# Heads that come out with tokens on partitions: batches 2 to 4 of an mLSTM cell followed by an FNet mix

## Chip, cores and metric

One core of a Trainium2 chip runs the kernel, alone. The metric is the device time of one execution in microseconds; less is better. TensorE (PE) multiplies matrices, VectorE (DVE), ScalarE (ACT) and GpSimd (POOL) work on elements, and SyncE (SP) issues the transfers, one behind the other on one queue.

## The reference

```python
B, H, S, D = 4, 8, 768, 40
for t in range(S):                       # mLSTM cell, per batch and head
    m_new  = max(f_gate[t] + m, i_gate[t])
    f_stab = exp(f_gate[t] + m - m_new);  i_stab = exp(i_gate[t] - m_new);  m = m_new
    C = f_stab * C + i_stab * outer(v[t], k[t])
    n = f_stab * n + i_stab * k[t]
    y[t] = sigmoid(o_gate[t]) * (C @ q[t]) / max(abs(n @ q[t]), 1.0)
x = y.transpose(0, 2, 1, 3).reshape(B, S, 320)
u  = x + real(fft(fft(x, axis=1), axis=2))           # FNet mix
un = (u - mean(u)) / sqrt(var(u) + 1e-6)             # over the 320 features
out = u + relu(un @ w_ch1) @ w_ch2                   # 320 -> 1280 -> 320
```

All inputs and the output are float32 (the two weights arrive as 64-bit floats and are converted on the core).

## The kernel before

**Stages.** Each batch passes through three stages: the mLSTM (functions `mlstm_*`, and `halves_*` for batches 2 to 4), the mix (`mix_*`) and the MLP (`mlp_*`). In the code a batch `b` counts from 0, a chunk `c` from 0 to 5 (128 tokens each). The gates of all batches are worked out once, at the start (`gates`), with batch and head on 32 partitions and the 768 tokens along them.

**The mLSTM of a chunk.** In place of the loop over tokens stands the chunked form: a weight matrix W of keys against queries (exponentials of gate sums, masked, times the scores k·q), applied to v, plus the state C applied to the decayed queries qg. In batches 2 to 4 a chunk is worked in two halves of 64 tokens, with TensorE products in 64x64 quarters of the array. Per chunk, in the order of the plan (`plan_halves`, slot s of the chunk): load of q, k, v and of the row maxima into W (`mlstm_load`, `mlstm_load_max`, slot s-5), load of the decays into Gb (`mlstm_load_decay`), `mlstm_scale_v` on POOL (s-1), the exponentials on ACT in two calls (`mlstm_exp`, slots s and s+1), `halves_scores` and `halves_to_state` on TensorE (s), the mask on POOL (`mlstm_mask`, s+1), the query scaling on POOL (`mlstm_scale_q`, s+1), the state's decay on POOL and addition on DVE (`halves_decay`, `halves_add`), the weighing on DVE (`halves_weigh`, s+2), then `halves_from_state` and `halves_from_chunk` on TensorE (s+3; the second half of the chunk products stands behind `halves_between`, a copy of one element by ACT).

The heads come out with features on partitions and tokens along them. ACT copies them to a buffer `hT` (`mlstm_heads`), TensorE turns them with four transposes (`halves_turn`, form `ph<-ident,h`), and DVE divides and gates them (`mlstm_finish`) into `x`, with tokens on partitions.

**The order of tokens.** The mix folds token t with token 768-t, so chunks 2, 4 and 5 are written backwards (`BACKWARDS`). Chunk borders lie at multiples of 128, and the fold needs some first tokens in another chunk than the one they are computed in; `mlstm_heads` moves these rows by copies of one column (`h_first`, `before[first]`).

**The mix.** `mix_fold` adds and subtracts the pairs of chunks (0,5), (1,4), (2,3); batches 3 and 4 fold a second time (`mix_fold_again`), with edits of single rows by POOL. TensorE transforms along tokens (`mix_seq`, `mix_tail`: tiles pz, pzt) and along features (`mix_feat`: pu), DVE adds (`mix_add`), ACT centers (`mix_center`), TensorE turns the result (`mix_turn`: put) for the MLP.

**What sets the order.** Every engine runs its queue in order. The order is a plan written by hand: `at(slot, phase, function, ...)`, run by slot and, within a slot, by phase (EVAC 0, FILL 1, MAIN 2, FILL_PE 3, with fractions). The MLP of batch 1 begins at slot 31 and fixes the slots of what follows; the mLSTM of batch 2 begins at slot 32, that of batches 3 and 4 at 50 and 82, and lies between the MLP products of the batch before.

**The gates' outputs for batches 2 to 4.** `maxima_out` stores the maxima in one transfer (M_d) and the decays (G_d) at slot 12; `halves_of_chunks` works out the exponentials of the halves (32x384), turns them by 6 transposes and DVE copies them to `colT` and `decB`.

Of the kernel before, what the change touches and what calls it, by code (L numbers as in the profile page):

```python
# [10 lines left out]
FP = mybir.dt.float32  # L11
# [26 lines left out]
NK = HALF + 1  # L38


BACKWARDS = (2, 4, 5)
PAIRS = ((0, 5), (1, 4), (2, 3))
# [10 lines left out]
def kernel(  # L53
# [11 lines left out]
    spread: bass.AP,  # L65
    out: bass.AP,
# [36 lines left out]
    h_first = const.tile([L, NP, 1], FP, name="h_first")  # L103
# [12 lines left out]
    hT_bufs = [const.tile([L, NP, L], FP, name=f"h{n}") for n in range(2)]  # L116
# [24 lines left out]
    def gates(gp):  # L141
        f_sb = gp.tile([BH, NT, L], FP, name="f_sb")
        a = gp.tile([BH, NT, L], FP, name="a")
# [42 lines left out]
        for t in hT_bufs + Cd_bufs:  # L186
            nc.gpsimd.memset(t, 0.0)

# [115 lines left out]
        def maxima_out():  # L304
            nc.sync.dma_start(out=M_d.rearrange("c i p t -> p c i t"), in_=M[0:BH].rearrange("p c (i t) -> p c i t", i=2))
            nc.sync.dma_start(out=G_d[:, H:].rearrange("c p t -> p c t"), in_=g[H:BH])

        def halves_of_chunks(step):


            half, end = M[0:BH, :, LH:], M[0:BH, :, LH - 1:LH].to_broadcast([BH, NT, LH])
            if step == 0:
                late["G"], late["K"] = (gp.tile([BH, NT, LH], FP, name=n) for n in ("G2", "K2"))
                nc.gpsimd.tensor_tensor(out=late["G"], in0=end, in1=half, op=OP.subtract)
                nc.gpsimd.tensor_tensor(out=late["K"], in0=a[:, :, 0:LH], in1=end, op=OP.subtract)
            elif step == 1:
                nc.scalar.activation(out=g[0:BH, :, LH:], in_=late["G"], func=AF.Exp)
                nc.scalar.activation(out=wk[:, :, 0:LH], in_=late["K"], func=AF.Exp)
            elif step == 2:
                d2 = late["dec2"] = w2_sb[0:BH, 0, 0:BH // 2 * NS].rearrange("p (n c) -> p n c", c=NS)  # L320
                ends = g[0:BH].rearrange("p c (i t) -> p (c i) t", i=2)[:, :, LH - 1]
                nc.gpsimd.tensor_tensor(out=d2, in0=ends.unsqueeze(1).to_broadcast([BH, BH // 2, NS]),
                                        in1=spread_sb[:, L:].unsqueeze(2).to_broadcast([BH, BH // 2, NS]), op=OP.mult)
            elif step == 3:
                p2 = bank("p2", [L, NT * BH + BH // 2 * NS], 2)
                pt, pd = p2[:, 0:NT * BH], p2[:, NT * BH:]
                late["p2"] = [t.rearrange("p (n c) -> p n c", c=n) for t, n in ((pt, BH), (pd, NS))]
                for c in range(NT):
                    nc.tensor.transpose(late["p2"][0][:, c, :], wk[:, c, :], ident[0:BH, 0:BH])
                nc.tensor.matmul(late["p2"][1], spread_sb[:, 0:L], late["dec2"], start=True, stop=True)  # L330
            else:
                pt, pd = late["p2"]
                nc.vector.tensor_copy(out=colT[:, :, 1, H:], in_=pt[:, :, H:])
                nc.vector.tensor_copy(out=decB[:, NP:], in_=pd[:, NP:])

        at(12, FILL + 0.7, maxima_out)
# [10 lines left out]
        for n, (s, phase) in enumerate(((8, FILL + 0.55), (10, FILL + 0.75), (12, FILL + 0.5), (17, FILL_PE + 0.5),  # L347
                                        (18, FILL + 0.75))):
            at(s, phase, halves_of_chunks, n)
# [90 lines left out]
    def mlstm_queries(b, c):  # L440
        return slice(LH if b > 0 and c == 0 else 0, L)

    def mlstm_load_decay(b, c):
        k, t = chunks[b, c], mlstm_queries(b, c)
        if (b, c) != (0, 0):
            k.Gb = gbp.tile([L, NP, L], FP, name="Gb", tag="Gb")
            for hip in range(2):
                h = slice(hip, H, 2) if b == 0 else slice(b * H + hip * NP, b * H + (hip + 1) * NP)
                nc.sync.dma_start(out=k.Gb[hip * 64:hip * 64 + 64, :, t],
                                  in_=G_d[c, h, t].unsqueeze(0).to_broadcast([64, NP, t.stop - t.start]))  # L450
# [14 lines left out]
    def mlstm_scale_q(b, c):  # L465
        k, t = chunks[b, c], mlstm_queries(b, c)
# [15 lines left out]
    def mlstm_mask(b, c):  # L482
        for i in range(2):
            W = chunks[b, c].W[i * LH:(i + 1) * LH]
            nc.gpsimd.affine_select(out=W, in_=W, compare_op=OP.is_ge, fill=0.0, base=0, pattern=[[0, H], [1, LH]],  # L485
                                    channel_multiplier=-1)
# [60 lines left out]
    def mlstm_gather(b, c):  # L547
        k = chunks[b, c]
        k.hT = hT_bufs[(b * NT + c) % 2]
# [4 lines left out]
        mlstm_heads(b, c, k.ph, c == 0)  # L554
        mlstm_tanh(b, c)

    def mlstm_heads(b, c, ph, parts=False):

        k = chunks[b, c]
        hT, before = k.hT, hT_bufs[(b * NT + c - 1) % 2]  # L560
        if b > 0:
            hT, before = (t.rearrange("p (hip m) t -> p hip m t", hip=2) for t in (hT, before))
        every, first, later = (tuple([slice(None)] * (len(ph.shape) - 1) + [t]) for t in
                               (slice(0, L), slice(0, 1), slice(1, L)))
        if c in BACKWARDS:
            nc.scalar.copy(out=hT[later], in_=backwards(ph, L - 1, L - 1))
            if c > TG:
                nc.scalar.copy(out=hT[first], in_=ph[first])
            else:
                nc.gpsimd.tensor_copy(out=k.hT[:, :, 0:1], in_=h_first)  # L570
        else:
            for r in (slice(hip * 64, hip * 64 + D1) for hip in range(2)) if parts else (slice(0, L),):
                nc.scalar.copy(out=hT[r], in_=ph[r])
            if c == 0:
                nc.gpsimd.tensor_copy(out=h_first, in_=k.hT[:, :, 0:1])
        if 0 < c < TG:
            nc.scalar.copy(out=before[first], in_=ph[first])
# [14 lines left out]
    def side(n):  # L592
        return banks["heads"].rearrange("p hip (s m t) -> p s hip m t", s=2, t=L)[:, n]

    TILES = ((0, 0), (1, 1), (0, 1), (1, 0))

    def columns(c, n):

        return LH if c == 0 else n

    def halves_scores(b, c):
# [5 lines left out]
        for p in range(NP):  # L607
            for hip, i in TILES:
                r, t = slice(hip * 64, hip * 64 + D), slice(i * LH, (i + 1) * LH)
                product(k.ps[t, hip, p, :], k.qk[r, 1, p, t], k.qk[r, 0, p, t], True)  # L610

    def halves_to_state(b, c):
        k = chunks[b, c]
        for p in range(NP):
            for i, hip in TILES:
                if 2 * c + i < NS - 1:
                    r, h, n = slice(i * LH, (i + 1) * LH), hip * NP + p, columns(c, D)
                    product(k.pc[hip * 64:hip * 64 + n, i, p, :], k.k[r, h * D:h * D + n], k.vw[r, h, :], True)

    def halves_state(k, i):  # L620
        return k.C[i][:, 0:NP * D1].rearrange("p (m d) -> p m d", d=D1)

    def halves_decay(b, c, i):

        k, n = chunks[b, c], 2 * c + i
        if 0 < n < NS - 1:
            nc.gpsimd.tensor_tensor(out=halves_state(k, i + 1), in0=halves_state(k, i),
                                    in1=decB[:, b * NP:(b + 1) * NP, n].unsqueeze(2).to_broadcast([L, NP, D1]), op=OP.mult)

    def halves_add(b, c, i):  # L630

        k, n = chunks[b, c], 2 * c + i
        if n == 0:
            nc.vector.tensor_copy(out=halves_state(k, 1), in_=k.pc[:, 0])
        elif n < NS - 1:
            nc.vector.tensor_tensor(out=halves_state(k, i + 1), in0=halves_state(k, i + 1), in1=k.pc[:, i], op=OP.add)

    def halves_weigh(b, c):
        k = chunks[b, c]
        W = k.W.rearrange("p (hip m) t -> p hip m t", hip=2)  # L640
        nc.vector.tensor_tensor(out=W, in0=k.ps, in1=W, op=OP.mult)

    def halves_from_state(b, c):

        k = chunks[b, c]
        k.ph = side(0)
        for m in range(2):
            for i in range(2):
                for hip, e in TILES:
                    if 2 * c + i > 0:  # L650
                        r, t, p = slice(hip * 64, hip * 64 + D), slice(i * LH, (i + 1) * LH), 2 * m + e
                        product(k.ph[e * 64:(e + 1) * 64, hip, m, t], k.C[i][r, p * D1:p * D1 + LH], k.qg[r, p, t],
                                m == 0 and i == (c == 0))

    def halves_from_chunk(b, c, turn):

        k = chunks[b, c]
        for m in range(2):  # L660
            for i, e in TILES:
                hip, n = i ^ turn, columns(c, D1)
                r, h = slice(i * LH, (i + 1) * LH), hip * NP + 2 * m + e
                product(k.ph[e * 64:e * 64 + n, hip, m, r], k.v[r, h * D1:h * D1 + n], k.W[r, h, :], False)

    def halves_between(b, c):

        nc.scalar.copy(out=warm[0:1, 0:1], in_=chunks[b, c].ph[0:1, 1, 1, L - 1:L])  # L668

    def halves_gather(b, c):  # L670
        k = chunks[b, c]
        k.hT = hT_bufs[(b * NT + c) % 2]
        mlstm_heads(b, c, k.ph)

    def halves_turn(b, c):
        k = chunks[b, c]
        px = side(0 if c == NT - 1 else 1)
        for p in range(NP):
            nc.tensor.transpose(px[:, p // 2, p % 2], k.hT[:, p, :], ident)  # L679
        k.px = px  # L680

    def mlstm_finish(b, c):
# [4 lines left out]
        px = k.px.rearrange("p (a pr) t -> p a pr t", a=2) if b == 0 else k.px  # L687
        h1 = px.rearrange("p a pr (two e) -> p a (pr two) e", two=2)
# [755 lines left out]
```

## Time and profile before

| | |
|---|---|
| median of 3 runs | 415.76 us (414.93, 415.76, 416.84) |
| profiled execution, span from the first to the last instruction | 413.2 us; the page gives no other time for this execution |
| granted TensorE clock, mean | 0.996 |
| DMA | 43.29 MB, mean 105 GB/s |

One core, so there is one span. "x" gives a count of instructions; a form "40*64 40x64" is stationary operand and moving operand, partitions by columns; in brackets stands how long the engine was idle before, and what released it. A float32 matmul is two instructions in the trace, a transpose one. In the timeline the first column is the start, the second the modelled duration.

### The profile page before, as it was taken

The numbers are of one execution on the slowest core, as the hardware profiler recorded it, in microseconds if no ns is written. First come the engines' busy times: TensorE is split into PE (matmuls) and PEld (weight loads), VectorE is DVE, ScalarE is ACT, GpSimd is POOL, SyncE is SP. The second block draws the span as 40 slices with busy tenths as digits, with TensorE's granted clock in tenths as the row PEclk, the third lists the DMA queues.
The fourth block names the chain that finished last, engine by engine and source line by source line (L and its number), as shares of the span: only waits on it lengthen the run. The fifth ranks groups of instructions, "written<-read, shape, count | busy, mean of one in ns | idle before, by whom it ended". The sixth has DMA issues, their size and how long they took to land.

```text
span 413.2 us, 10648 instructions
## 1 busy us (share of the span) xinstructions
PE 391.4 (95%) x4246; PEld 284.4 (69%) x4246; DVE 280.5 (68%) x669; ACT 181.9 (44%) x510; POOL 130.1 (31%) x227
## 2 busy tenths in 40 slices
PE   8998899989999999998999998897999999999997
PEld 6777555546567677754559997864559888556996
DVE  7789886778749558665865688756854786335652
ACT  6986257486641133653553333454550123455000
POOL 6673403448873243152053531443040000020000
PEclk9999999999999999998999999999999999999999
DMA  7969578386863445354001444300000000000010
GB/s 216 293 194 313 130 197 248 103 250 217 207 172 107 116 121 140 112 157 136 0 2 44 134 139 129 95 19 3 0 2 0 33 32 34 0 0 2 24 41 32
DMA packets 23836, 43.29 MB, mean 105 GB/s; under 512 B 5076, under 2 KB 12972, under 8 KB 23660
## 3 DMA queue, kind: packets, MB, share of 16 engines
q1 hardware_dynamic: 23788, 42.63, 35.4%
q8 instruction: 33, 0.54, 0.6%
q14 instruction: 15, 0.12, 0.1%
HBM read 38.49 MB, written 4.12 MB: 103 GB/s over the span
## 4 chain that ended last, share of the span: by engine, by line
PE 66%; POOL 9%; DVE 8%; DMA 7%; issue 7%; SPq 1%; ACT 1%; POOLq 0%; DVEq 0%; ACTq 0%
PE po L1201 19%; PE pm L1082 15%; PE po L1145 8%; PE pm L1087 5%; POOL qg L472 3%; PE ph L489 3%; PE pu L899 3%; POOL W L485 3%; DMA dd_sb<-in_dft_d 2%; PE ps L489 2%; DMA raw<-in_w 2%; PE pz L868 2%; PE pz L856 1%; DMA so<-in_o 1%; PE ph L679 1%
## 5 line engine op out<-in xcount | busy, mean ns | idle before, releaser
L1151 DVE SCALAR_TENSOR_TENSOR x<-po,rstd,x 128x160 f32<-128x160 f32 (+1 forms) x69 | 26.9, 394 | 41.3 <-PE po L1201 36.8
L485 POOL TENSOR_SCALAR_AFFINE_SELECT W<-W 64x512 f32<-64x512 f32 x36 | 25.0, 694 | 91.7 <-ACT W L462 77.1
L1091 DVE TENSOR_TENSOR h<-h,pm 128x384 f32<-128x384 f32 x60 | 30.9, 550 | 32.3 <-PE pm L1082 17.7
L462 ACT ACTIVATE W<-W,colT 128x64 f32<-128x64 f32 x144 | 38.3, 344 | 0.0
L1082 PE MATMUL pm<-uT,w_sb 128*128 128x384 f32 x90 | 37.9, 509 | 0.2 <-DVE uT L1070 0.2
L1145 PE MATMUL po<-w_sb,h 128*128 128x320 f32 x120 | 34.4, 435 | 0.0
L1020 PE MATMUL pm<-uT,w_sb 128*128 128x384 f32 x80 | 29.6, 499 | 0.1
L1145 PEld LDWEIGHTS po<-w_sb,h 128*128 128x128 f32 x120 | 22.2, 190 | 9.4 <-issue 0.6
L1201 PE MATMUL po<-T,S 128*128 128x160 f32 x180 | 27.9, 302 | 0.2 <-DVE x L1151 0.2
L1201 PE MATMUL po<-w_sb,h 128*128 128x160 f32 x180 | 26.7, 301 | 1.5 <-DVE x L1151 1.5
L472 POOL TENSOR_TENSOR qg<-qk,Gb 128x512 f32<-128x512 f32 (+1 forms) x21 | 27.7, 1321 | 0.8 <-DMA Gb<-G_d 0.6
L1087 PE MATMUL pm<-uT,w1t_sb 64*128 64x384 f32 x120 | 26.9, 511 | 0.4 <-DVE h L1091 0.4
L1201 PEld LDWEIGHTS po<-w_sb,h 128*128 128x128 f32 x180 | 25.1, 190 | 3.0 <-DVE x L1151 2.1
L1201 PEld LDWEIGHTS po<-T,S 128*128 128x128 f32 x180 | 25.5, 190 | 1.8 <-DVE x L1151 0.5
L668 ACT COPY warm<-ph 1x1 f32<-1x1 f32 x18 | 2.6, 147 | 53.5 <-PE ph L489 51.1
L1082 PEld LDWEIGHTS pm<-uT,w_sb 128*128 128x128 f32 x90 | 15.7, 191 | 12.6 <-DVE h L1091 3.6
L966 POOL TENSOR_TENSOR t<-rstd 128x6 f32<-128x6 f32 x12 | 3.8, 316 | 65.0 <-DVE v L960 64.5
L1138 ACT ACTIVATE h<-h 128x384 f32<-128x384 f32 x45 | 23.2, 521 | 2.0 <-DVE h L1091 2.0
L947 ACT COPY uT<-put 128x384 f32<-128x384 f32 x24 | 11.1, 477 | 25.6 <-PE put L942 25.6
L478 POOL TENSOR_TENSOR vw<-kvt,colT 128x328 f32<-128x328 f32 x23 | 21.2, 920 | 3.3 <-DVE shift L200 3.0
L1087 PEld LDWEIGHTS pm<-uT,w1t_sb 64*128 64x128 f32 x120 | 13.0, 185 | 13.2 <-issue 8.2
L935 ACT ACTIVATE uc<-x 128x384 f32<-128x384 f32 x24 | 14.5, 613 | 16.2 <-DVE x L927 15.2
(233 smaller groups left out, 882.0 us busy)
## 6 DMA issues: line engine op xcount, KB each, us to landing
kvt<-in_kv SPq DMA_DIRECT2D x24, 336.0 KB
qk<-in_qkT SPq DMA_DIRECT2D x48, 160.0 KB
raw<-in_w SPq DMA_DIRECT2D x10, 640.0 KB
Gb<-G_d SPq DMA_DIRECT2D x36, 128.0 KB
W<-M_d SPq DMA_DIRECT2D x36, 128.0 KB
so<-in_o SPq DMA_DIRECT2D x24, 160.0 KB
out<-x SPq DMA_DIRECT2D x24, 160.0 KB
ds_sb<-in_dft_s SPq DMA_DIRECT2D x1, 1155.0 KB
```

The lines of the kernel that those rows point to most:

```text
L462: nc.scalar.activation(out=k.W[:, h, :], in_=M, func=AF.Exp, scale=-1.0, bias=colT[:, c, 0, b * H + h:b * H + h + 1])
L472: nc.gpsimd.tensor_tensor(out=k.qg[:, :, t], in0=k.qk[:, 0, :, t], in1=k.Gb[:, :, t], op=OP.mult)
L478: nc.gpsimd.tensor_tensor(out=k.vw, in0=k.v1, in1=colT[:, c, 1, b * H:(b + 1) * H].unsqueeze(2).to_broadcast([L, H, D1]), op=OP.mult)
L485: nc.gpsimd.affine_select(out=W, in_=W, compare_op=OP.is_ge, fill=0.0, base=0, pattern=[[0, H], [1, LH]], channel_multiplier=-1)
L1020: nc.tensor.matmul(k.pm[i], w1_sb[:, ch, f0:f0 + L], u[2 * ch], start=(ch == 0 and not ahead), stop=(ch == 1 and ahead), skip_group_check= ...
L1082: nc.tensor.matmul(bank, w, u, start=start, stop=True, skip_group_check=True)
L1087: nc.tensor.matmul(bank, block(w1t_sb, i)[rows], mlp_u(gr, 1)[rows], start=False, stop=True, skip_group_check=True)
L1091: nc.vector.tensor_tensor(out=h, in0=h, in1=bank, op=OP.add)
L1138: nc.scalar.activation(out=h, in_=h, func=AF.Relu, scale=-1.0)
L1145: nc.tensor.matmul(k.po, hidden(gr, f)[:, i * L:(i + 1) * L], w2_sb[:, f, :], start=(f == 0), stop=(f == NFF - 1))
L1151: nc.vector.scalar_tensor_tensor(out=u, in0=po, scalar=k.rstd[:, c:c + 1], in1=u, op0=OP.mult, op1=OP.add)
L1201: nc.tensor.matmul(po, a[:, f], w[:, f], start=start and f == 0, stop=f == half - 1, skip_group_check=True)
```

## The change

- **Heads with tokens on partitions (batches 2 to 4).** In `halves_from_state` and `halves_from_chunk` the operands swap roles: the queries (or W) are stationary, 64 wide, and the state (or v) moves, 41 columns. The result needs no turn; `halves_turn`, `halves_gather` and the head copies of these batches go, and `mlstm_finish` reads the heads' bank. The bank has two sides, used by even and odd chunks. All of the chunk products now stand behind `halves_between`.
- **Chunk borders.** Chunks begin at tokens 1, 128, 256, 385, 513 and 640 (`START`); chunks 1 and 4 hold tokens 0 and 384 as their first. Inputs are laid out for this by the host, and two chunks per batch get eight more products for the first token (`alone`). A new input (`in_heads`, tile `sp_sb`) brings what these need; `halves_start` makes the first state.
- **Gates of the halves.** `gates_of_halves` takes the place of `maxima_out` and `halves_of_chunks`: it shifts the maxima by copies on ACT, forms two 32x768 differences on POOL, three exponentials on ACT, stores M_d in twelve transfers and G_d in one (slot 17), and turns columns by two groups of 24 products; ACT copies them out.
- **Plan.** Exponentials at s-1 and s, mask at s, query scaling at s-2, weighing at s+1, loads at s-6, finish at s+4. Batches 3 and 4 begin at slots 51 and 83. In batch 1 the turn of chunk 3 moves from slot 14 to 16.
- **Mix.** The special row moves from the pair (2,3) to (1,4); the transforms have 386 columns instead of 385; the second fold has no edits of single rows. The pool of the gates' tiles is closed at slot 28 instead of 15.

```diff
+START = (1, L, 2 * L, HALF + 1, HALF + L + 1, HALF + 2 * L)
+SPECIAL = {1: 0, NT - 2: NS // 2}
...
+        def gates_of_halves(step):
+            W, G, K = keep, shift, f_sb
...
+            elif step == 1:
+                m, w = flat_of(M), W.rearrange("p c (i t) -> p c i t", i=2)
+                nc.scalar.copy(out=W[:, 0:4:3].rearrange("p c t -> p c t"),
+                               in_=bass.AP(tensor=m.tensor, offset=m.offset + 1, ap=[list(m.ap[0]), [HALF, 2], [1, L]]))
+                nc.scalar.copy(out=W[:, 1], in_=M[0:BH, 1])
...
+                nc.gpsimd.tensor_copy(out=W[:, 0:4:3, L - 1:L], in_=late["nexts"][:, 1:5:3])
+                nc.gpsimd.tensor_copy(out=W[:, 4, LH:LH + 1], in_=late["nexts"][:, 5])
             elif step == 2:
...
+                nc.gpsimd.tensor_tensor(out=g2, in0=halves(late["starts"]), in1=w, op=OP.subtract)
...
+            elif step == 3:
+                for t in (G, K, late["between"]):
+                    nc.scalar.activation(out=t, in_=t, func=AF.Exp)
+                nc.sync.dma_start(out=sp_sb, in_=first_heads)
...
+            elif step in (5, 7):
+                n = BH - H
+                p2 = bank("p2", [L, 2 * NT * n + (BH // 2 * NS if step == 5 else 0)], 2)
...
+            else:
+                j = (step - 6) // 2
+                cols = colT[:, :, j, H:].rearrange("p c (b hip m) -> p c b hip m", hip=2, m=NP)
+                for hip in range(2):
+                    nc.scalar.copy(out=cols[:, :, :, hip], in_=late["pt"][:, hip, :, :, hip])
+                if j == 0:
+                    nc.scalar.copy(out=decB[:, NP:], in_=late["pd"][:, NP:])
...
+        def state(C, q, hip, i, p, start=False):
+            r = slice(hip * 64, hip * 64 + D)
+            product(k.ph[half(i ^ back(c)), hip, p, :], q[r, p], C[r, p * D1:(p + 1) * D1], start)
+
+        for p in range(NP):
+            for hip, i in TILES:
+                state(k.C[i], k.qg[:, :, half(i)], hip, i, p, p == 0)
+        if c in SPECIAL:
+            for p in range(NP):
+                for hip in range(2):
+                    state(states[(b * NS + SPECIAL[c]) % len(states)], alone[int(c > 1)], hip, back(c), p)
...
-            at(s + 1, FILL - 0.5, mlstm_exp, b, c, NP)
-            at(s + 1, FILL, mlstm_mask, b, c)
-            at(s + 1, FILL + 0.1, mlstm_scale_q, b, c)
-            at(s + 2, FILL, halves_weigh, b, c)
+            at(s + 1, FILL, halves_weigh, b, c)
             at(s + 3, MAIN - 0.1 if end else FILL_PE, halves_from_state, b, c)
-            at(s + 3, MAIN - 0.1 if end else FILL_PE, halves_from_chunk, b, c, 0)
             at(s + 3, MAIN if end else FILL_PE + 0.5, halves_between, b, c)
-            at(s + 3, FILL_PE + 3, halves_from_chunk, b, c, 1)
...
+            at(s + 3, FILL_PE + 3, halves_from_chunk, b, c)
             at(s + 3, FILL + 0.35, mlstm_tanh, b, c)
+            at(s + 4, (MAIN if c == 1 else FILL) + 0.05, mlstm_finish, b, c)
```

## The prediction

> **What bounds the kernel now.** I read the page first, then TensorE's own timeline around one chunk, the groups by form, TensorE's waits, all engines' timelines at those waits, and last the stretch in which batch 1 hands over to the MLP (30 to 64 us).
>
> ```profile
> span 413.2 us, 10648 instructions
> ...
> PE 391.4 (95%) x4246; PEld 284.4 (69%) x4246; DVE 280.5 (68%) x669; ACT 181.9 (44%) x510; POOL 130.1 (31%) x227
> ```
>
> TensorE is the bound, so the change is worth the TensorE time and the TensorE waits that it removes. The second column below is modelled and overlaps; the cost of a group is its start to the next group's start.
>
> ```profile
> 118.39 0.69 PE L489 MATMUL ps<-qk 40*64 40x64 f32 x32
> 118.90 0.63 PE L489 MATMUL ps<-vw,kvt 64*64 64x41 f32 x32
> 119.34 0.41 PE L489 MATMUL ph<-W,kvt 64*41 64x64 f32 x16
> ...
> 142.65 0.69 PE L489 MATMUL ph<-qg,C 40*64 40x64 f32 x32
> 143.17 0.41 PE L489 MATMUL ph<-W,kvt 64*41 64x64 f32 x16
> 143.39 0.65 PE L489 MATMUL ps<-qk 40*64 40x64 f32 x32
> 143.86 0.49 PE L489 MATMUL ps<-vw,kvt 64*40 64x41 f32 x32
> 144.17 0.41 PE L489 MATMUL ph<-W,kvt 64*41 64x64 f32 x16
> 144.51 0.38 PE L865 MATMUL pzt<-ds_sb,fe 128*64 128x193 f32 x1
> ...
> 245.61 0.60 PE L679 MATMUL ph<-ident,h 128*128 128x128 f32 x4
> 246.04 0.49 PE L942 MATMUL put<-ident,uc 128*128 128x128 f32 x3
> ```
>
> Here stand all prices of a chunk: state products 0.52 us, chunk products 0.22 and 0.34, turns 0.43. The pair at 118.90 and 143.86 differs only in the width of the stationary operand, 64 against 40: 0.44 against 0.31 us.
>
> ```profile
> PE ph L489 <- POOL qg L472: 4.9, 4, 2.1
> PE po L1201 <- DVE x L1151: 3.1, 3, 1.5
> PE ph L489 <- DVE W L641: 1.4, 1, 1.4
> PE ph L679 <- ACT W L462: 0.8, 1, 0.8
> ```
>
> Waits of TensorE that chunk work causes. The largest is the same in batches 3 and 4:
>
> ```profile
> 277.90 1.07 ACT L462 ACTIVATE W<-W,colT 128x64 f32<-128x64 f32 x4
> 279.04 1.38 POOL L485 TENSOR_SCALAR_AFFINE_SELECT W<-W 64x512 f32<-64x512 f32 x2 [4.34 <-ACT W L462]
> 280.50 1.38 POOL L472 TENSOR_TENSOR qg<-qk,Gb 128x512 f32<-128x512 f32 x1
> 281.94 0.70 PE L489 MATMUL ph<-qg,C 40*64 40x64 f32 x32 [2.07 <-POOL qg L472]
> ```
>
> Exponentials, mask and the decayed queries run one behind the other, and TensorE waits 2.07 us for the last.
>
> **TensorE's work.** (1) The turns go: 18 chunks x 0.43 = -7.7. (2) State and chunk products cost 0.52 + 0.22 + 0.34 = 1.08 a chunk. The new ones have 41 moving columns but 64-wide stationary operands. Bounds for 32 of them: 0.31 (40-wide, 41 columns) and 0.52 (64 columns); I take 0.44, the row of their very form. Twice 0.44 and the change of array form at the end (0.34 - 0.22 = 0.12) make 1.00: -0.08 for 15 chunks. The three first chunks cost 0.88 now (half of the state products are missing there) and gain 0.12 each. Sum -1.2 + 0.4 = -0.8; by the bounds -6 to +1.4. (3) Six chunks get 16 instructions for a first token. They fill two quarters of the array, not four, so twice 0.44/32 each: 6 x 0.44 = +2.6; 1.3 if four overlap, 5.3 if none do. Sum of work: -5.9.
>
> [...] The rows show 41 columns at 0.31 where the stationary operand is 40 wide, so here the 64-wide operand holds the time. [...]
>
> **TensorE's waits.** The scaling of the queries moves from slot s+1 to s-2, the second exponentials and the mask from s+1 to s. The chain above then ends some two slots before its products. What goes: in the timeline at 82 to 86 us 0.24 + 1.44 + 0.23 = 1.9; at 112 to 116, 0.80 (that wait belongs to a turn) + 0.49 = 1.3; at 186 and 280, 2 x 2.07 = 4.1. After the wait at 186 the table by stretches shows PEclk 0.65, 0.50, 0.50, 0.65 in the four us from 189: some 3.4 us at half rate, 1.7 lost, which I count as gone. The two waits for DVE (1.55 at 251, 1.33 at 264) come from a residual that stands behind sums, a finish and a weighing in DVE's order; the change only reorders these, so half: -1.4. Sum -10.4. What is late next: the weighing, now one slot behind its scores, and the whole of the chunk products, which now stand behind ACT's one-element copy (before, half did). That copy held TensorE up once, 0.23 us, in 18 chunks; bounds 0 and 18 x 0.23 = 4.1; I take +1.0, near the one row.
>
> [...]
>
> **The handover of batch 1.** This is where the change pays. Now:
>
> ```profile
> 45.62 0.58 ACT L566 COPY h<-ph 128x508 f32<-128x508 f32 x1 [2.77 <-PE ph L530]
> ...
> 46.32 0.66 PE L587 MATMUL px<-ident,h 128*128 128x128 f32 x4 [0.81 <-ACT h L568]
> ```
>
> ACT's copy of the last chunk (c=5) lets it be turned, and the transform of tokens follows. The new gate work (gates_of_halves) stands ahead of this copy on ACT: four copies of maxima and three exponentials, which wait for POOL's two subtractions of 32x768. Working: the tanh of c=4 ended at 42.8; TensorE's wait of 1.30 ahead of the turn of c=3 (36.74) goes, as that turn moves from slot 14 to 16, so 41.5. Four copies at 0.35 (rows 0.30 and 0.58): 42.9. Two small POOL copies at 0.2: 43.3. Two subtractions, each twice the 32x384 row of 0.83: 46.6. The exponential of the second, twice 0.51, and a small one of 0.2: 47.8 against 45.62, +2.2. Behind the turn TensorE gets 2 x 24 products (48 instructions each, 64-wide, two quarters busy: 27.5 ns, 1.3 us a group; 0.7 if four overlap, 2.6 if none), the spread of the decays (0.5, the row at 43.36) and, between the groups, a wait for the bank that ACT's three copies free (3 x 0.3 + 0.2 = 1.1). 2.6 + 0.5 + 1.1 = 4.2. Behind it wait the token transform, the feature transform and the MLP. Together +6.4; from 3.0 (four overlap, -1.2; the copy of c=5 no later than now, -2.2) to 13.9 (worked out under the rivals).
>
> **What I cost at nothing.** The stores of the maxima go from one at slot 12 to twelve at slot 17, with sp_sb and G_d: 14 issues at 0.42 on SP's queue, and behind them batch 2's first loads, now issued at 38.35. These land ten us or so later; first use is the query scaling in slot 30, after 57. SP then stands until 53.07 for a weight piece anyway. If that cover goes, each us of lateness counts. The W loads one slot sooner wait for the chunk products three chunks back, with Gb and so queued behind; five slots are left. The finish reads the heads' bank instead of the turned copy, in the same forms (0.15 to 0.49 each). ACT loses 18 head copies (0.58 each), DVE two copies, POOL the one-row edits of the second fold; POOL gains a start state (0.53) per batch and small copies at 31% busy. One more column of the transforms is 0.3% of them, under 0.1 us. The gates' memory is held until slot 28; who takes it over first writes in slot 47.
>
> **Sum.** -5.9 - 10.4 + 1.0 + 6.4 = -8.9 on the span of 413.2: 404.3. The median of the runs, 415.76, lies 2.6 above that span; with the same margin 406.9 us.
>
> **Rivals.** *Handover hidden:* four quarters overlap and ACT's copy is no later than now (handover 3.0), both DVE waits go (-1.4), no new wait (-1.0): 406.9 - 5.8 = 401.1. For it: TensorE starts the last chunk's products about 1 us sooner. Against: ACT keeps its order, so the copy of c=5 can't pass the exponentials. *Waits move:* the 10.4 come back elsewhere, because the finish now reads right behind the chunk products and DVE is 68% busy: -5.9 + 6.4 = +0.5, 416.3. Against: POOL, which ended the largest waits, gets two slots of slack. *Slower:* ACT's block at the handover. If POOL's subtractions take twice the row (+3.3; the 128x328 product ranges from 0.73 to 1.97), the small products don't overlap (+2.6) and the 1.3 plus the start 0.3 aren't gained (+1.6), the handover is 13.9; with half of the waits removed -5.9 - 5.2 + 1.0 + 13.9 = +3.8, 419.6. With half of the waits it decides from a handover of 10.1 on, with all of them from 15.3.
>
> **Chances.** Forecast 0.55, hidden 0.20, waits move 0.12 (most of it within 0.5%, about 2.1 us, which is what a measurement here can tell from no change), slower 0.13. Faster: 0.55 + 0.20 + 0.03 = 0.78; same 0.07; slower 0.02 + 0.13 = 0.15. The range from 400 (the hidden case and some of term 2's bound) to 416.5 leaves out the slower case and a little below.
>
> **What would show it.** No turn left in batches 2 to 4; per-chunk state products at 0.44; no POOL qg among TensorE's waits; ACT's copy of c=5 near 48; the MLP's first matmul near 67, not 60.9. I am wrong if that last is past 71, or if DVE or ACT end TensorE waits of over 5 us after it.

## Result, and the profile after

| | before | after |
|---|---|---|
| median | 416.30 us (8 runs) | 420.23 us (8 runs, 418.30 to 422.43) |
| span of the profiled execution | 413.2 us | 420.1 us |
| granted clock, mean, of that execution | 0.996 | 0.967 |

The ratio is 1.0104 (95% interval 1.0072 to 1.0137): slower by 1%, where a faster kernel, 406.9 us, had been predicted. The page:

```profile
span 420.1 us, 10967 instructions
...
PE 398.2 (95%) x4408; PEld 291.4 (69%) x4408; DVE 282.5 (67%) x668; ACT 173.8 (41%) x488; POOL 132.5 (32%) x233
...
PEclk9999659996999999999999999899999999999999
```

The last line is the new thing: the granted clock is low in the fifth and sixth slice (42 to 63 us), in the tenth (95 to 105) and in the 26th (263 to 273). TensorE's timeline at the handover of batch 1, where the prediction put its largest cost:

```profile
41.36 1.07 PE L591 MATMUL ph<-W,kvt 128*41 128x128 f32 x16
46.68 1.08 PE L642 MATMUL px<-ident,h 128*128 128x128 f32 x4 [4.24 <-DVE x L761]
47.56 2.78 PE L917 MATMUL pz<-ds_sb,fe 128*128 128x386 f32 x4
50.27 2.76 PE L383 MATMUL p<-ident,a 32*64 32x24 f32 x48
52.96 1.00 PE L388 MATMUL p<-w_sb,spread_sb 32*128 32x192 f32 x2
54.57 2.75 PE L383 MATMUL p<-ident,f_sb 32*64 32x24 f32 x48 [0.61 <-ACT decB L396]
57.26 1.55 PE L917 MATMUL pzt<-ds_sb,fe 128*64 128x386 f32 x4
...
71.98 1.24 PE L1069 MATMUL pm<-uT,w_sb 128*128 128x384 f32 x3
```

The turn of c=5 starts at 46.68, only 0.36 us later than before, but TensorE idles 4.24 us ahead of it: the products of the last chunk end sooner than they did, while ACT's exponentials still stand in front of the head copy, and DVE's fold of pair (2,3) in front of the finish of c=4. Its first two steps took 1.53 + 1.31 us, where the same steps took 0.72 + 0.17 at 42.20 before; they run beside POOL's two subtractions, but that these stretched them was not tested.

```profile
41.51 1.46 POOL L349 TENSOR_TENSOR shift<-starts,keep 32x768 f32<-32x768 f32 x1
41.80 1.53 DVE L835 TENSOR_TENSOR eo<-x 128x320 f32<-128x320 f32 x1
42.94 1.70 POOL L351 TENSOR_TENSOR f_sb<-a,ends 32x768 f32<-32x768 f32 x1
43.36 1.31 DVE L838 COPY fe<-eo 128x2 f32<-128x2 f32 x1
44.68 0.84 ACT L355 ACTIVATE f_sb<-f_sb 32x768 f32<-32x768 f32 x1 [0.83 <-POOL f_sb L351]
45.53 0.56 ACT L629 COPY h<-ph 128x512 f32<-128x512 f32 x1
46.04 0.49 DVE L761 TENSOR_TENSOR x<-px,so 128x320 f32<-128x320 f32 x1
```

Between 44.4 and 61.4 us the clock is 0.5 throughout, and the rows take up to twice their time (the products at 47.56 take 2.78 us, in run 1 at a whole clock 1.47). The first MLP matmul starts at 71.98 instead of 60.87.

By stretches (columns: busy time and count of each engine, then the clock, the DMA share, GB/s):

```profile
36.00:42.00 6.00, 5.06 (x72) 4.45 (x73) 4.65 (x15) 4.65 (x17) 2.72 (x8) 1.00 0.90 357
42.00:48.00 6.00, 1.76 (x13) 1.42 (x10) 5.62 (x10) 2.62 (x5) 5.84 (x7) 0.70 0.25 67
48.00:54.00 6.00, 5.96 (x54) 3.81 (x52) 5.59 (x15) 0.00 (x1) 1.47 (x5) 0.50 0.63 165
54.00:60.00 6.00, 5.43 (x56) 4.19 (x57) 2.75 (x3) 0.86 (x5) 3.17 (x3) 0.50 0.83 230
```

TensorE's waits name what else is new:

```profile
PE po L1250 <- DVE x L1200: 4.8, 2, 4.0
PE px L642 <- DVE x L761: 4.2, 1, 4.2
PE ph L550 <- ACT warm L741: 2.7, 2, 1.7
PE ph L550 <- DVE x L761: 1.4, 1, 1.4
```

The waits for POOL's decayed queries are gone, as predicted. In their place stand a residual that comes 3.97 us late at 261.5, and ACT's one-element copy, 1.70 us late at 94.2. Behind each of these the clock fell again, to 0.50 (266.2 to 269.6 and 95.6 to 102.4). DVE's timeline tells why the residual is late:

```profile
258.80 0.68 DVE L758 SCALAR_TENSOR_TENSOR so<-so,den 128x320 f32<-128x320 f32 x1
262.44 0.49 DVE L761 TENSOR_TENSOR x<-ph,so 128x320 f32<-128x320 f32 x1 [2.96 <-DMA out<-x]
...
265.01 0.87 DVE L1200 SCALAR_TENSOR_TENSOR x<-po,rstd,x 128x160 f32<-128x160 f32 x2
```

The finish of a chunk of the last batch comes four slots sooner than before. It writes into the x buffer that the batch two before is still being stored from, waits 2.96 us for those stores, and the residual stands behind it (with two sums, 0.81 and 1.27 us, between).

The balance, 420.1 - 413.2 = +6.9. Up to the first MLP matmul +11.1: of the 17.07 us of half clock, 17.07 - 2.3 - 0.6 (waits) = 14.1 are work, so 7.1 are lost to the clock, if all of that work takes twice its time; 4.0 are the rest. From there on -4.2: half clock 5.1 against 1.7 (half of the stretches' length), +3.4; waits of over 0.2 us 10.5 against 11.6, -1.1; what is left for TensorE's own work is -6.5.

### The profile page after: what moved, and what is told of

Read it like the earlier page. It is cut to its first block, busy times and chain, and to the rows that moved or that the text cites. A ratio compares the mean times of both kernels' runs of the same rounds, so it can differ in the third digit from the quotient of the medians.

```text
span 420.1 us, 10967 instructions
## 1 busy us (share of the span) xinstructions
PE 398.2 (95%) x4408; PEld 291.4 (69%) x4408; DVE 282.5 (67%) x668; ACT 173.8 (41%) x488; POOL 132.5 (32%) x233
## 4 chain that ended last, share of the span: by engine, by line
PE 56%; issue 16%; DVE 14%; POOL 9%; DMA 2%; SPq 1%; ACT 0%; POOLq 0%; DVEq 0%
PE po L1250 17%; PE pm L1131 14%; PE pm L1136 5%; POOL W L546 3%; POOL qg L531 2%; PE ph L550 2%; POOL C L698 2%; PE pu L948 1%; POOL vw L537 1%; PE pz L905 1%; DMA out<-x 1%; PE pM L230 1%; DVE so L758 1%; PE p L383 1%; PE pz L917 1%
## 5 line engine op out<-in xcount | busy, mean ns | idle before, releaser
L546 POOL TENSOR_SCALAR_AFFINE_SELECT W<-W 64x512 f32<-64x512 f32 x36 | 28.0, 777 | 63.8 <-ACT W L521 62.4
L1131 PE MATMUL pm<-uT,w_sb 128*128 128x384 f32 x90 | 37.7, 506 | 0.2 <-DVE uT L1119 0.2
L521 ACT ACTIVATE W<-W,colT 128x64 f32<-128x64 f32 x144 | 37.4, 339 | 0.0
L1250 PE MATMUL po<-T,S 128*128 128x160 f32 x180 | 28.8, 308 | 4.8 <-DVE x L1200 4.8
L698 POOL TENSOR_TENSOR C<-C,decB 128x164 f32<-128x164 f32 x33 | 16.5, 501 | 49.0 <-DVE C L705 47.6
L1069 PE MATMUL pm<-uT,w_sb 128*128 128x384 f32 x80 | 31.5, 532 | 0.1
L531 POOL TENSOR_TENSOR qg<-qk,Gb 128x512 f32<-128x512 f32 x21 | 27.6, 1316 | 4.8 <-DMA Gb<-G_d 4.8
L996 ACT COPY uT<-put 128x384 f32<-128x384 f32 x24 | 11.1, 479 | 36.9 <-PE put L991 36.9
L705 DVE TENSOR_TENSOR C<-C,ps 128x164 f32<-128x164 f32 x33 | 10.5, 319 | 23.1 <-PE ps L550 13.4
L1136 PE MATMUL pm<-uT,w1t_sb 64*128 64x384 f32 x120 | 25.2, 510 | 0.7 <-DVE h L1140 0.7
L1131 PEld LDWEIGHTS pm<-uT,w_sb 128*128 128x128 f32 x90 | 15.5, 189 | 13.7 <-DVE h L1140 4.9
L1069 PEld LDWEIGHTS pm<-uT,w_sb 128*128 128x128 f32 x80 | 15.3, 204 | 10.5 <-issue 3.4
```

What stands on the lines that cost most here:

```text
L521: nc.scalar.activation(out=k.W[:, h, :], in_=M, func=AF.Exp, scale=-1.0, bias=colT[:, c, 0, b * H + h:b * H + h + 1])
L531: nc.gpsimd.tensor_tensor(out=k.qg[:, :, t], in0=k.qk[:, 0, :, t], in1=k.Gb[:, :, t], op=OP.mult)
L698: nc.gpsimd.tensor_tensor(out=halves_state(k.C[i + 1]), in0=halves_state(k.C[i]), in1=decB[:, b * NP:(b + 1) * NP, n].unsqueeze(2).to_broa ...
L1069: nc.tensor.matmul(k.pm[i], w1_sb[:, ch, f0:f0 + L], u[2 * ch], start=(ch == 0 and not ahead), stop=(ch == 1 and ahead), skip_group_check= ...
L1131: nc.tensor.matmul(bank, w, u, start=start, stop=True, skip_group_check=True)
L1136: nc.tensor.matmul(bank, block(w1t_sb, i)[rows], mlp_u(gr, 1)[rows], start=False, stop=True, skip_group_check=True)
```

## The experiments

The theories. **A**: the wait ahead of the turn of c=5 brings the clock down, and that is most of the loss; this was refined after the first run to **A'**: a stretch of the small gate products counts like a wait. Rival **B**: the gate products and their order cost the time themselves. **C**: the sooner finish runs into the stores. **D**: ACT's one-element copy stands behind too much of ACT's work.

Every run lists its span and mean clock, which gives a second measure, an estimate that takes work at half clock to last twice as long: span x (1 - clock) is the time that the half clock can have cost (an upper bound, as some of it fell on waits), span x clock the span without it. In two executions of the same instructions the low stretches differ (at the handover 17.1 us in the changed kernel's profile, 3.4 + 6.8 in that of the run with late finishes, which has the same instructions there), so the medians are read, not one profile:

| kernel | median us | ratio to before (95%) | span x clock | lost at most |
|---|---|---|---|---|
| before (25 runs, beside numbers 1 to 4) | 416.1 | | 412.3 | 3.3 |
| after | 420.2 | 1.0104 (1.0072 to 1.0137) | 406.3 | 12.3 |
| idle products in the wait | 416.7 | 1.0023 (0.9995 to 1.0050) | 406.4 | 8.7 |
| turn first | 418.6 | 1.0054 (1.0028 to 1.0080) | 405.5 | 11.5 |
| late finishes in the last batch | 415.4 | 0.9982 (0.9948 to 1.0016) | 404.9 | 8.0 |
| state products sooner | 426.4 | 1.0235 (1.0169 to 1.0302) | 411.5 | 12.7 |
| idle products, gate products later | 417.3 | 1.0008 (0.9980 to 1.0036) | 407.0 | 8.7 |
| before, with small products | 420.1 | 1.0106 (1.0053 to 1.0158) | 414.2 | 4.2 |
| ACT's order | 420.1 | 1.0097 (1.0061 to 1.0132) | 408.4 | 10.0 |
| four edits together | 410.5 | 0.9871 (0.9825 to 0.9918) | 404.9 | 3.7 |
| ... gate products mixed with idle ones | 413.6 | 0.9947 (0.9912 to 0.9982) | 410.0 | 1.9 |
| ... without the idle products | 412.5 | 0.9902 (0.9869 to 0.9935) | 404.0 | 5.8 |
| ... tanh sooner | 413.0 | 0.9919 (0.9890 to 0.9948) | 406.2 | 5.1 |
| ... gate products in eight parts | 409.3 | 0.9853 (0.9824 to 0.9881) | 405.3 | 2.6 |

Its first two rows say it in short: by this measure the change is worth 6.0 us without the half clock, and the half clock takes up to 9.0 more than it did.

**1. Idle products in the wait.**

```diff
-for s, phase, n in ((24, 5.5, 1), ...
+for s, phase, n in ((18, 0.9, 9), (24, 5.5, 1), ...      # idle_products(n)
```

> The changed kernel with nine idle products (128x256 matmuls on a spare bank, 0.43 us each, results unused) put ahead of the turn of c=5, so that TensorE has work in the 4.24 us in which it waits for DVE and ACT there. Nothing that anybody waits for is moved. Theory A (the clock): the loss at the handover is above all the half clock from 44.5 to 61.6 us, brought on by that wait; with TensorE kept busy the granted clock stays at 1.0 there, and of the 14.3 us of work that ran at half rate about 7 come back: some 413, ratio to the kernel before about 0.994, first MLP matmul near 64.8 instead of 71.98. Rival B (the work): the new gate work itself and its order cost the 11 us; the first MLP matmul stays near 72, and the time at 420 or above.

416.7, first MLP matmul at 68.42. Work that nobody waits for made the kernel 3.5 us faster, so the clock was part of it; but half of what A expected. TensorE's timeline and its stretches show the rest:

```profile
46.93 1.47 PE L917 MATMUL pz<-ds_sb,fe 128*128 128x386 f32 x4
48.32 1.58 PE L383 MATMUL p<-ident,a 32*64 32x24 f32 x48
49.83 0.59 PE L388 MATMUL p<-w_sb,spread_sb 32*128 32x192 f32 x2
51.03 2.46 PE L383 MATMUL p<-ident,f_sb 32*64 32x24 f32 x48 [0.61 <-ACT decB L396]
```

```profile
42.00:48.00 6.00, 5.83 (x30) 4.41 (x26) 5.62 (x10) 2.62 (x5) 5.84 (x7) 1.00 0.26 70
48.00:54.00 6.00, 5.39 (x102) 4.40 (x102) 5.58 (x15) 0.86 (x5) 1.37 (x5) 0.79 0.62 157
54.00:60.00 6.00, 6.00 (x20) 3.10 (x16) 2.52 (x3) 0.23 (x1) 3.15 (x3) 0.64 0.84 251
```

The wait is filled and the clock whole until 51.4. Then it falls for 6.8 us, with no wait of over 0.61 us before it: what stood there are the small products. That gave A'.

**2. Turn first.** The exponentials (with their stores) behind the head copy of c=5, the fold behind the finish of c=4.

```diff
-(17, FILL + 0.75), (18, FILL + 0.8)      # steps 3, 4
+(18, FILL + 0.77), (18, FILL + 0.8)
-done = ((17, 19, 22) if b == 0
+done = ((18, 19, 22) if b == 0
```

> The changed kernel with two things in another order, no work added or removed: ACT's three exponentials of the gates (step 3, with its stores) behind the head copy of c=5, and DVE's fold of the pair (2,3) behind the finish of c=4. Theory A: the turn of c=5 then starts near 43.5 instead of 46.68, no wait of over 2 us is left ahead of it or of the token transform, the clock stays whole, and the time falls by 7 (half clock) and 2 to 3 (the wait): 410 to 412. Rival B (the work): only the wait's 2 to 3 us come back: 417 to 418. If the fold is now what the token transform waits for, by more than 2 us, the clock falls all the same and the time stays near 420.

418.6, between the second case and the third. The turn starts at 42.88 and the first MLP matmul at 68.36, but the token transform now waits 2.08 us for the fold, and the small products follow it at once. In this profile the clock is low from 47.0 for 10.2 us; in the median the loss hardly moved (11.5). Only part of the wait came back.

**3. Late finishes in the last batch.**

```diff
-at(s + 4, (MAIN if c == 1 else FILL) + 0.05, mlstm_finish, b, c)
+at(s + (5 if end else 8), FILL + 0.05, mlstm_finish, b, c)    # b == 3
-(14, 17, 20)
+(18, 21, 22)                                                  # its folds, b == 3
```

> The changed kernel, with the finishes of the last batch (b=3) put back to the slots that they had before the change (eight slots behind the chunk's scores instead of four; five for c=5) and its folds with them. Theory C: the sooner finish writes into the x buffer that batch b=1 is still being stored from; DVE waits for those stores (1.91 us at 244.7, 2.96 us at 262.4), and the residual behind it holds TensorE for 3.97 us at 261.5 and costs it 3.4 us of half clock at 266.4. With late finishes these go: -4 (of 3.97 + 0.80 + 1.7 some 1 to 2 us come back as the small DVE waits that the kernel before had there, 1.55 and 1.33), so near 416. Rival: DVE is late there anyhow by its order (sums, weighing, residual), and the wait only moves: within 1 us of 420.

415.4, as C expected. The waits for the residual fell from 4.8 to

```profile
PE po L1253 <- DVE x L1203: 1.8, 1, 1.8
```

and no low stretch is left behind 97.4 us in its profile but the end. The edit moves the whole finish, so DVE's own 1.7 us for it left this place together with the wait of 2.96 for the stores; the run does not tell the two apart, the rows at 258.80 and 262.44 above do.

**4. State products one slot sooner**, with the copy of ACT.

```diff
-at(s + 3, ... FILL_PE, halves_from_state, b, c)
+at(s + 2, ... FILL_PE, halves_from_state, b, c)          # and halves_between
```

> The changed kernel with the state products and the one-element copy of ACT one slot sooner for all chunks but the last of a batch (slot s+2 instead of s+3); the chunk products stay. Theory D: the waits of 1.70 us at 94.2 and 0.99 us at 122.9, and the half clock from 95.7 to 102.5 us (3.4 us lost), come from that copy standing behind other work of ACT; they go. Against it stand 15 more changes of array form at 0.12 us each (1.8): net -3 to -4.5, near 416. Rival: ACT is late by its whole queue (conversions of weight pieces, exponentials), and what comes behind it is waited for instead: no more than -1, the time near 420.

426.4, slower by 6. D's wait is gone, and a worse one has come:

```profile
PE ph L550 <- DVE x L761: 8.1, 6, 3.2
```

The state products now wait for the finish of the chunk before, which DVE reaches only in that slot, behind two passes over a weight piece (1.60 and 1.02 us at 95.6). The change's own place for them, one slot later, is better.

**5. Idle products, and the gate products later** (slots 24 and 25 instead of 19 and 20, in a score bank).

```diff
-(19, FILL_PE + 0.5), (20, FILL + 0.75), (20, FILL_PE + 0.5), (21, FILL + 0.75)
+(24, FILL_PE + 5.4), (25, FILL + 0.75), (25, FILL_PE + 5.4), (26, FILL + 0.75)
```

> The run with nine idle products ahead of the turn of c=5, and in addition the two groups of small gate products (48 instructions each, stationary 32x64, 24 columns) and ACT's copies of them moved from ahead of the token transform's tails to between the turns of the feature transform (slots 24 and 25), where TensorE gets idle products anyway; their bank is one of the free score banks. Same work. In the run with idle products alone the clock still fell, from 51.4 to 58.3 us, with no wait of over 0.61 us before it, right behind the small products. Theory A' (small products count as idle for the clock): dense products alone stand there now, the clock stays whole until slot 24, 3.4 us come back, and 0.6 for the wait on ACT's copy: near 412.7. If they bring it down in slots 24 and 25 as well, only the 0.6: near 416. Rival B (the products' own time is all they cost, 2.6 to 3.2 us): within 1 us of 416.7.

417.3, the second of A's cases, and by time alone not to be told from B. The clock of this profile tells them apart: it is whole where it was low, and low where the products went, from 60.8 on for 10.2 us:

```profile
48.00:54.00 6.00, 6.00 (x26) 2.72 (x26) 5.58 (x14) 1.19 (x3) 2.09 (x4) 1.00 0.55 147
54.00:60.00 6.00, 5.68 (x67) 3.85 (x65) 5.76 (x13) 3.30 (x6) 1.53 (x2) 1.00 0.87 245
60.00:66.00 6.00, 6.00 (x65) 4.81 (x62) 4.54 (x10) 1.86 (x7) 0.45 (x1) 0.56 1.01 234
```

**6. The kernel before, with small products** (two groups of 24 matmuls, 48 instructions each, unused).

```diff
+nc.tensor.matmul(pw[i % 2 * LH:(i % 2 + 1) * LH, 0:24], ident[0:BH, 0:LH], ident[0:BH, 8:BH], ...)   # x24, twice, slot 18
```

> The kernel before the change, with 96 small products of the gates' form (stationary 32x64, 24 columns, a result that nobody uses) put behind the first products of the token transform, where the change has its own. Nothing else is touched. By their own time at full clock they cost 96 x 27.5 ns = 2.6 us. Theory A': the granted clock falls behind them although TensorE does not wait, for one or two windows of 3.4 us: 1.7 to 3.4 us more, 4.3 to 6.0 in all, ratio 1.010 to 1.014. Rival B: 2.6 us and a whole clock, ratio 1.006.

3.5 us slower by the medians, between the two expectations, and the interval holds both. In the profile they take 3.2 us, and from their last part on the kernel that had a whole clock there has 6.8 us of half clock (50.9 to 57.8) without a wait:

```profile
48.41 3.26 PE L144 MATMUL pi<-ident 32*64 32x24 f32 x96
...
53.09 2.93 PE L874 MATMUL pz<-ds_sb,fe 128*128 128x385 f32 x4
```

(2.93 where this group took 1.56.) Over four runs the loss grew from 2.5 (16 runs of the kernel before, beside it) to 4.2, half of what a stretch of 6.8 us would add in each. Two of the four have a clock of 0.992, no lower than the kernel before often shows, so the clock does not fall in every execution.

**7. ACT's order:** the tanh a slot sooner, the conversions of weight pieces behind the copy of their slot.

```diff
-at(s + 3, FILL + 0.35, mlstm_tanh, b, c)
+at(s + 2, FILL + 0.35, mlstm_tanh, b, c)
-((s, 0.7), (s + 1, 0.7), (s + 2, 0.6))       # take, convert, join; the conversion at slot 35 likewise
+((s, 0.7), (s + 2, 2.6), (s + 3, 0.6))
```

> The changed kernel with ACT's order mended instead of TensorE's: the tanh of a chunk one slot sooner (s+2), and ACT's conversions of the weight pieces behind the one-element copy of their slot instead of ahead of it (their joins one slot later). Theory D: the waits of 1.70 us at 94.2 and 0.99 at 122.9 fall below 0.4 each and the half clock behind the first (6.8 us, 3.4 lost) goes: 2 to 5.5 us, so 415 to 418. Rival: the conversions are only pushed into the next slot's exponentials, and the wait appears there: within 1 us of 420.

420.1, the rival. No wait for the copy is left; TensorE's waits now have

```profile
PE ph L550 <- DVE x L761: 2.9, 2, 1.5
PE ps L550 <- DVE C L705: 2.4, 3, 1.1
```

where they had 1.4 and 0.2. What ACT did late, DVE now does late. D names the wait rightly and not what bounds it.

**8. Four edits together:** 2, 3, the later gate products of 5, and five idle products behind the turn (`(18, 1.5, 5)`).

> The changed kernel with four edits that each answer a loss found so far: exponentials behind the copy and fold behind the finish (turn of c=5 first), five idle products behind that turn, the small gate products in slots 24 and 25, and late finishes in the last batch. Theories A and C together: first MLP matmul near 63 us, a clock that is whole but for the waits in batch 2, some 343 us from there to the end: a span of 406, time 408, ratio 0.98. Rival B: the handover keeps its 11 us, and only the late finishes count: 415, ratio 0.998.

410.5, ratio 0.987: faster than both kernels. The first MLP matmul starts at 64.87, a little later than expected (63), and a low stretch of 3.4 us stands at 63.1, right behind the second group of gate products (61.2 to 62.7).

**9. The gate products of 8 mixed with idle ones**, one ahead of every 12 instructions.

```diff
 for c in range(NT):
+    if c % 3 == 0:
+        idle_products(1)
```

> The version with the four edits together (idle products behind the turn, late finishes, turn first, gate products in slots 24 and 25), with its small gate products broken up: a dense idle product (128x256) ahead of every 12 instructions of them, eight in all where three idle products stood in two of the slots' turns, so six more and 2.6 us more work at most. Theory A' (a stretch of only small products brings the clock down): the half clock behind slot 24 (3.4 us at 63 there) goes, 1.7 to 3.4 us come back, and the time stays within 1.5 us of that version's 410.5 with a granted clock of 0.996 or more. Rival: the clock falls by the time since the last wait or by the small products' number, however they are spaced: 412 to 413, clock 0.99.

The clock is whole from the start to 92.4 us, and in the median of ten runs 0.9955, the highest of the changed kernels; three runs had 1.000. That is A', not the rival, though dense work was added here too. The time missed: 413.6. Start to start, an idle product between small ones costs 0.63 us, not the 0.45 of five in a row (43.47 to 45.71), and the MLP starts at 69.2.

```profile
59.17 0.53 PE L385 MATMUL p<-ident,a 32*64 32x24 f32 x12
59.63 0.70 PE L145 MATMUL pi<-rest 128*128 128x256 f32 x2
60.26 0.53 PE L385 MATMUL p<-ident,a 32*64 32x24 f32 x12
60.72 0.70 PE L145 MATMUL pi<-rest 128*128 128x256 f32 x2
```

**10. Number 8 without the idle products behind the turn.**

```diff
-((18, 1.5, 5), (24, 5.5, 1), ...
+((24, 5.5, 1), ...
```

> The version with the four edits together, without the five idle products behind the turn of c=5. TensorE then waits some 2 us for DVE's fold between the turn and the token transform, with dense products behind it and no small ones near. If a wait of 2 us is enough for the clock, it falls near 46 us for one window or more and the time is 1.7 to 5 us above 410.5 (412 to 415); if the small products were needed as well, the clock stays whole there and the time is within 0.5 us of 410.5, as nobody waits for the idle products.

412.5, and the low clock is back where nothing but a wait stands:

```profile
43.05 0.66 PE L642 MATMUL px<-ident,h 128*128 128x128 f32 x4 [0.74 <-ACT h L629]
45.78 2.94 PE L920 MATMUL pz<-ds_sb,fe 128*128 128x386 f32 x4 [2.08 <-DVE fe L845]
```

The group at 45.78 takes 2.94 instead of 1.57; the stretch is 44.8 to 51.6. So here a wait of 2.08 us, with one of 0.74 and 0.6 us of turns ahead of it, was enough without any small product. In all ten runs the clock is 0.988 or lower (0.986 to 0.992 in the four runs with the idle products); by time alone the two are not told apart, as their intervals overlap.

The same profile limits A'. The two groups of 48 small products stand in it unbroken, and the clock stays whole (1.00 from 54 to 72 us):

```profile
60.03 1.58 PE L383 MATMUL p<-ident,a 32*64 32x24 f32 x48
63.02 1.58 PE L383 MATMUL p<-ident,f_sb 32*64 32x24 f32 x48
```

```profile
60.00:66.00 6.00, 5.99 (x111) 4.89 (x110) 5.71 (x13) 2.95 (x11) 0.74 (x1) 1.00 0.98 232
```

In numbers 8 and 11 (next) the same groups are followed by 3.4 and 10.2 us of half clock. So small products in one piece were followed by half clock in those two profiles and not in this one.

**11. Number 8 with the tanh alone sooner** (the first edit of 7).

> The version with the four edits together, with the tanh of each chunk of batches 2 to 4 one slot sooner (s+2 instead of s+3), the conversions of the weight pieces left where they are. The one-element copy then has one 0.46 us instruction less ahead of it: the waits of 1.70 and 1.00 us in batch 2 fall to 1.24 and 0.54, and the half clock behind the first (3.4 us) may go: 0.9 to 2.6 us, 408 to 409.6. Rival: ACT meets the tanh a slot sooner in another full slot and the exponentials come later: within 0.5 us of 410.5.

413.0: no gain, the rival or worse. The wait at 90.9 fell from 1.70 to 1.35, but one of 0.29 grew to 0.83 (at 108.5) and the one behind DVE's finish from 1.44 to 1.80. Part of the loss need not be the tanh's: this profile has 10.2 us of half clock behind the gate products (59.9 to 70.1), that of number 8 has 3.4 with the same instructions there.

**12. The gate products of 8 in eight parts** of 12 instructions between the dense products of slots 20 to 26, one idle product fewer. In the trace the last two parts stand together (24 instructions at 63.74).

```diff
+SPLIT = {5: ((22, 4.5), (23, 4.5), (24, 5.4)), 7: ((25, 5.6), (26, 5.4), (26, 5.6))}
+for step, slots in SPLIT.items():
+    for (slot, phase), p in zip(slots, ((0, 3), (1, 0), (1, 3))):
+        at(slot, FILL_PE + phase, lambda step=step, p=p: late[step](*p))     # three chunks of one half
...
```

> The version with the four edits together, with its small gate products in eight parts of 12 instructions between the dense products of the two transforms (slots 20 to 26) instead of two stretches of 48, and one idle product fewer; no dense work is added. Theory A' (a stretch of only small products brings the clock down): the clock stays whole from the start to the first wait of batch 2, at 0.995 or more in the median of the runs, the first MLP matmul starts at 63.5 or sooner (64.9 before), and the time is 408.5 to 410, ratio 0.981 to 0.985; each change of array form may cost 0.1 us (the mixed version showed 0.2 for each of its idle products beyond their own time), at most 1 us in all. Rival (the number of small products counts, however they stand): half clock near 60 as before, 410.5 to 411.5.

409.3, ratio 0.9853: the lowest median here, 6.1 us below before by the ratio, though its interval overlaps that of number 8. The clock is whole from the start to 89.3 us with the same small products and no dense work added:

```profile
48.00:54.00 6.00, 5.35 (x34) 2.71 (x32) 5.59 (x15) 0.88 (x2) 1.48 (x5) 1.00 0.63 165
54.00:60.00 6.00, 6.00 (x55) 3.83 (x51) 5.70 (x11) 3.36 (x7) 1.87 (x2) 1.00 0.89 236
60.00:66.00 6.00, 6.00 (x77) 4.34 (x74) 5.30 (x12) 3.61 (x11) 0.74 (x1) 1.00 0.95 216
```

The MLP starts at 64.55, not at 63.5, so the expected time was just met; the median clock is 0.9935, as a low stretch still follows the wait of 1.71 us at 86.8, in batch 2.

## Why the prediction was wrong

The sum expected -8.9 on the span, the profiles show +6.9. By its own terms the miss of 15.8 us is: TensorE's work -0.6, waits +6.6, clock +12.2, handover without the clock -2.4. So the step that failed most is the clock, priced at one gain of 1.7 us and at nothing for every new wait; the next is the finish, moved four slots sooner and costed at nothing.

*TensorE's work, -5.9:* right in size, -6.5 as what the balance leaves. The turns are gone (-7.7). The state and chunk products cost 0.49 + 0.58 = 1.07 a chunk against 1.08, not 1.00: narrowing them brought nothing. 32 products with the same 41 columns and a stationary operand 40 wide took 0.32 (271.00 to 271.32), so the columns alone do not set the time; what else does was not tested. The first tokens cost 0.44 a chunk, as worked out. These rows add up to -4.6; the other 1.9 of the balance were not traced to rows, so that the term came out so close is in part luck. The bounds of the second term, worked out again from the same rows, are -5.5 to +2.0, not -6 to +1.4.

*Waits that go, -10.4, and a new one, +1.0.* The chain behind the decayed queries went as described. But where the prediction asked what is late next it named only the weighing and ACT's copy. The copy cost 2.7 us, two and a half times its term. The finish, four slots sooner, was filed under work that moves at no cost: its write into an x buffer that is still being stored was not looked for. It holds a residual (4.8 us in two waits, of which run 3 took back 3.0), and the finish as a thing that state products wait for took another 1.4. Waits changed by -1.1 where -7.7 was expected (-10.4 + 1.0 without the 1.7 for the clock). Of these the finish is the larger miss. The rival "waits move" named it, for reading right behind the chunk products; that fits the 1.4, not the stores behind the 4.8.

*The clock, -1.7:* wrong in sign. It was priced once, at one wait of before. The change brought new low stretches, at the handover (7.1), behind the copy of ACT and behind the residual (5.1 with 1.7 before): +10.5 in the profiles; 12.3 against 3.3 at most, +9.0, in the medians.

*The handover, +6.4:* +11.1, of which 4.0 without the clock. So the terms were not too small. The copy of c=5 did not come 2.2 us later but 0.1 us sooner (45.53), though behind the exponentials, as described. The two groups took 2.76 and 2.75 us at half clock; at a whole clock the first took 1.5 (48.32 to 49.83 in run 1), against the 1.3 of the prediction; the wait between them 0.61 against 1.1. What failed was to cost these products at their time alone, and not to ask what a wait of four microseconds with 5 us of small products behind it does to everything after.

*The slower rival* (419.6) has the right place and, by luck, the right time, as its price is wrong: ACT's block, 13.9, from POOL's subtractions and non-overlapping products. POOL's subtractions took 1.46 and 1.70, as the prediction's 1.66 each; the block was 4.0, the rest was the clock. The marks set for being wrong, an MLP start past 71 and DVE or ACT ending over 5 us of waits behind it, were both reached (71.98; 4.8 + 2.7 + 1.4).

Left open: how to remove the copy's wait in batch 2. Runs 4, 7 and 11 each took part of it away, and DVE was late instead. In the changed kernel DVE is busy for 33.1 of the 42 us from 88 to 130 and ACT for 23.7, so neither is full there on the average; what in their order would have to change was not found. The stores that hold the finish were avoided by time, not with a third x buffer; that was not tried.

## What to carry to other kernels

A stretch with little matmul work can have half clock behind it, as here a wait of 2.08 us had in run 10 and 96 instructions with small tiles (3.26 us) in run 6, 6.8 us in both, and is priced with that: read the clock row slice by slice, and add span x (1 - clock) to the comparison of two kernels. If such products can't be avoided, try them in short pieces between dense ones: in the profiles here the same 96 instructions were followed by a low stretch in one or two pieces (3.4 to 10.2 us in runs 1, 5, 6, 8 and 11), with one exception (run 10), and by none in seven or eight (runs 9 and 12, one profile each). When a step moves sooner, ask for every buffer that it writes whether its last reader, a store too, is done by then.

## What the runs showed of the hardware

The low stretches read here in the profiles lasted 3.4, 6.8, 10.2 or 17.1 us (those at the very end apart): one, two, three and five times 3.41 us, a fifth of the 17.07 at the changed kernel's handover. They differed between executions of the same instructions (17.1 us there, 3.4 + 6.8 in run 3). A wait of 2.08 us was followed by 6.8 us of half clock in run 10, and so was, in run 1, a stretch of products of 32x64 with 24 columns in which the longest wait was 0.61 us. Neither was followed by it each time: of the kernel before's two waits of 2.07 us only one was, by 3.4 us, and the small products of run 10 were not. Why the stretches have these lengths no run shows, and which property of these products counts (32 rows, 64 columns or 24 moving ones) was not tested.
